# Attention with a routed expert layer on one core: k read in q's layout, full-row value products, and one timed list in place of a hand-ordered period

## The chip, the cores and the metric

The kernel is one program on one core of a Trainium2 chip. The metric is device time in microseconds (us). A core has a matmul engine (PE; its weight loads are PEld), a vector engine (DVE), an activation engine (ACT), a general engine (POOL) and a queue engine (SP). Each works through its own instructions strictly in program order and waits on semaphores for the others. DMAs are issued from SP, ACT and POOL and run on the core's 16 DMA engines.

## The reference

First a normalised attention over 8 batches of 12 heads, 448 positions, 64 channels, then a dense layer plus one chosen expert of eight for every token:

```python
q_n, k_n = rmsnorm(q, g_q), rmsnorm(k, g_k)          # over the 64 channels
scores = q_n @ k_n.T / sqrt(64)                       # per batch and head
attn = exp(scores) / sum(exp(scores))
x = (attn @ v) laid out as [8*448, 12*64]             # 3584 tokens x 768
y_dense = relu(x @ w1_dense) @ w2_dense               # 768 -> 512 -> 768
expert = argmax(x @ w_gate); gate = its softmax value
y = y_dense + gate * (relu(x @ w1[expert]) @ w2[expert])
```

The sum over keys does not depend on the order of the keys, as long as k and v are permuted alike.

## The kernel before, in words

**Groups and periods.** Four heads of a batch make a group `g`; there are 24 groups, three to a batch. `period(g)` holds the program of one group in seven steps `s`, and it works on several groups at once: the scores and exponentials of group g+1, the value products and divisions of group g, the PE transposes of k and q of group g+2, the norm statistics (14 `bn_stats` on DVE, L190) and the normalisation (4 products on POOL, L211) of group g+3, and loads of groups g+3 to g+6. In each step `scores` issues two to four matmuls (L247) and one exponential on ACT (L249, 896 values a partition), which sets the beat of the period. The PSUM tile of scores has two buffers, so ACT frees the place for the scores two steps on.

**Value products.** `attend(g, r, part)` multiplies the exponentials by the values for one half r of the group's heads. All its matmuls take 64 of the 128 rows; the two row halves alternate and write to different PSUM banks, and between part 0 and part 1 they change banks. `fenced()` puts a no-op on ACT there, which waits for part 0 and for which part 1 waits. The result lies in one PSUM tile, AV, which `division` (a reciprocal and two products on DVE, L313 and L309) must empty before the next `attend` starts.

**Loads.** q goes to partitions so that one partition holds seven neighbouring positions of a head (rows of 1792 bytes). k and v go in four DMAs for two groups, with three or four neighbouring positions a partition (rows of 768 and 1024 bytes), so that after the transposes each 128-key chunk of scores lies ready. All these loads are issued by SP. q has three buffers, k has two (each of two groups), v has one (of two groups); they lie in the space of the last five weight jobs (`LATE`), which are therefore loaded only when the attention's loads are over: all five in period 21, from POOL's queue.

**Routing.** When a batch is complete, `logits`, `choose`, `ranks`, `places` and `gates` find each token's expert and its place; `dense` and `relu` make the 512 hidden values of 128 tokens, and `scatter` (POOL, indirect DMA) writes the token's row to a table in device memory. PSUM tile W has two banks, shared by transposes, dense products, logits and ranks.

**Slot tiles.** The second part reads that table by experts, 128 slots a tile: `turn` loads a tile transposed (SP), `gemm1`, `htrans`, `gemm2` compute it on PE with ACT between, DVE copies the result (L677) and POOL scatters it to the output (L678). 14 tiles are known to be full after batch 5; `early_list` (20 small DVE instructions) finds them in one piece after period 20. After the last period `tail_and_slots` finishes the last two batches' work, makes the `final_list` and the `gaps`, and only then starts the tiles.

**Order.** Nothing reorders instructions: each engine's order is the order in which the Python code emits them.

Of the kernel before, what the change touches and what calls it, by code (L numbers as in the profile page):

```python
# [14 lines left out]
AX = mybir.AxisListType  # L15


@with_exitstack
def kernel(
# [92 lines left out]
    LATE, WPACE = 5, 1.75  # L112
    lflat = we.rearrange("p e a f -> p (e a f)")[:, -LATE * KD * F:]

    def lds(n, w):
        return lflat[:, n * 4 * S:(n + w) * 4 * S].bitcast(F32).rearrange("p (h s) -> p h s", h=2 * w)

    kls = [lds(0, 2), lds(2, 2)]
    qls = [lds(i, 1) for i in (4, 5, 6)]
# [21 lines left out]

    def load_q(g):
        if g < NG:
            xin["q", g] = qls[g % 3]
            nc.sync.dma_start(xin["q", g], q.rearrange("b h s d -> (b h) s d")[4 * g:4 * g + 4]
                              .rearrange("(i r) (p j) d -> (r p) i (j d)", r=2, j=J))

    def load_kv(x, src, g, n, engines):

        h = src.rearrange("b h s d -> (b h) s d")[4 * g:4 * (g + n)].rearrange(  # L150
            "(i r) s d -> r i s d", r=2)
        for r in range(2):
            for half in range(2):
                w = 4 if r == half else 3
                t0 = 0 if half == 0 else S - 64 * w
                c0 = 0 if r == 0 else S - w * D
                engines[(2 * r + half) % len(engines)].dma_start(
                    x[half * 64:half * 64 + 64, :, c0:c0 + w * D],
                    h[r][:, t0:t0 + 64 * w].rearrange("i (p t) d -> p i (t d)", t=w))

    def load_k(g):
        if g < NG:
            x = kls[g // 2 % 2]
            load_kv(x, k, g, 2, [nc.sync])
            for i in range(2):
                xin["k", g + i] = x[:, 2 * i:2 * i + 2]

    def load_v(g):
        if g < NG:
            load_kv(vls, v, g, 2, [nc.sync])  # L170
            for i in range(2):
                xin["v", g + i] = vls[:, 2 * i:2 * i + 2]
# [9 lines left out]
    def moments(g, name, s0, s1):  # L182
        weave(stats(g, name, s0, s1))
# [31 lines left out]
    def transposes(g):  # L215
        for n, name in enumerate("kq"):
            for s in range(J):
                c = S + (s if s < 3 else 6 if s == 3 else s - 1) * D if name == "k" else s * D
# [5 lines left out]

    def turned_q(g):
        qTs[g] = sb.tile([P, 2, S], BF16, tag="qT", name="qT")
        nc.vector.tensor_scalar(qTs[g], Wb[:, :, :S], gqk, None, op0=ALU.mult)

    def turned_k(g):

        kT = kTs[g % 2]
        nc.vector.tensor_copy(kT[:, :12 * D].rearrange("p (s c d) -> p c s d", c=2, d=D),
                              Wb[:, :, S:S + 6 * D].rearrange("p c (s d) -> p c s d", d=D))
        nc.vector.tensor_copy(kT[:, 12 * D:].rearrange("p (c d) -> p c d", d=D)[:, 0:3:2],
                              Wb[:, :, S + 6 * D:2 * S])

# [14 lines left out]
    def attend(g, r, part):  # L251


        va = vas[g % 3]
        if part == 1:
            fenced()
        full = (0, 1, 2) if r == 0 else (4, 5, 6)
        for s in full + (3,):
            for m in range(4):
                for half in range(2):  # L260
                    if s == 3 and half != r:
                        continue
                    hh = half ^ part
                    row = slice(half * 64, half * 64 + 64)
                    i = nc.tensor.matmul(  # L265
                        av[:, hh, m], exs[g, s][row, hh, QC[m]:QC[m] + P], va[row, s, hh, :De],
                        start=(part == 0 and s == full[0] and m == 0),
                        stop=(part == 1 and s == 3 if r == part else part == 1 and s == full[2]),
                        skip_group_check=True)
                    if part == 1 and fence[0]:  # L270
                        after(i, fence[0])
                        fence[0] = None
        if part == 0:
            fence[1] = i

    fence = [None, None]

    def fenced():
        if fence[1]:
            fence[0] = nc.scalar.nop()  # L280
            after(fence[0], fence[1])
            fence[1] = None

    def after(i, j):
        tc.add_manual_dep(i.ins, j.ins.name, mybir.DependencyInfo(
            mybir.DependencyClass.Sync, mybir.DependencyReason.DATA),
            reason="row tiles change banks")

    def weave(*works):

        works = [list(w) for w in works]
        while any(works):
            for w in works:
                if w:
                    w.pop(0)()

    def divide(g, r):
        weave(division(g, r))

    def division(g, r):  # L300
        b, gb = divmod(g, NB)
        if gb == 0 and r == 0:
            xas[b] = rb[b % 3][:, :, :XH].bitcast(BF16)
            xTs[b] = sb.tile([P, KD, S], BF16, tag="xT", name="xT")
        inv = sb.tile([P, 2, 4, 1], F32, tag="inv", name="inv")
        x = xas[b][:, :, gb * 256:gb * 256 + 256].rearrange("p m (a h i) -> p h m a i", a=2, h=4)

        def head(hh):
            nc.vector.tensor_tensor(  # L309
                x[:, 2 * hh + r], av[:, hh, :, :D].rearrange("p m (a i) -> p m a i", a=2),  # L310
                inv[:, hh].unsqueeze(3).to_broadcast([P, 4, 2, 32]), ALU.mult)

# [3 lines left out]
    def xtrans(g):  # L316
        b, gb = divmod(g, NB)
        for a in range(2):
# [4 lines left out]
    def xturned(g):  # L323
        b, gb = divmod(g, NB)
        nc.vector.tensor_copy(xTs[b][:, 2 * gb:2 * gb + 2],
                              Wb[:, 1, :2 * S].rearrange("p (a s) -> p a s", a=2))


    def logits(b):
# [154 lines left out]
    def dense(c, bank, k0, k1):  # L484
        b, m = divmod(c, 4)
        if b >= B:
            return
# [358 lines left out]
```

## Time and profile before

| | us |
|---|---|
| median of 3 runs (426.85 to 431.15) | 427.57 |
| the profiled execution | 427.64 |
| its span, first to last instruction | 425.9 |
| PE / DVE / ACT / POOL busy | 330.3 / 216.5 / 216.4 / 204.6 |
| first exponential of groups 0 and 2 | 17.3, 35.7 |
| last exponential | 249.7 |
| result copies of tile 1 and of the last tile (31) | 291.4, 413.7 |

A row of a group or of the timeline reads: source line, engine, operation, out<-in, shapes, count, then busy time and the mean of one, then the engine's idle time before it and what ended it. In the timeline the start and the length stand first, and neighbours of one kind are merged. A "q" after an engine's name means its sequencer, which issues DMAs. The ends of matmuls are modelled, so a row of n matmuls is longer by one matmul's latency than n times their pace.

### The profile page before, as it was taken

The numbers are of one execution on the slowest core, as the hardware profiler recorded it, in microseconds if no ns is written. First come the engines' busy times: TensorE is split into PE (matmuls) and PEld (weight loads), VectorE is DVE, ScalarE is ACT, GpSimd is POOL, SyncE is SP. The second block draws the span as 40 slices with busy tenths as digits, with TensorE's granted clock in tenths as the row PEclk, the third lists the DMA queues.
The fourth block names the chain that finished last, engine by engine and source line by source line (L and its number), as shares of the span: only waits on it lengthen the run. The fifth ranks groups of instructions, "written<-read, shape, count | busy, mean of one in ns | idle before, by whom it ended". The sixth has DMA issues, their size and how long they took to land. (4 is left out here: it accounts for less than half of the span.)

```text
span 425.9 us, 13310 instructions
## 1 busy us (share of the span) xinstructions
PE 330.3 (78%) x5170; PEld 200.7 (47%) x5219; DVE 216.5 (51%) x772; ACT 216.4 (51%) x345; POOL 204.6 (48%) x280
## 2 busy tenths in 40 slices
PE   0367777978878879779782876499999999999980
PEld 0135554554555545455451643135555555555540
DVE  4757686757877768587878343302212122221220
ACT  1287785966867868669772651113232232323310
POOL 2285585585677883857758312316322221212220
PEclk9998898979999989999998899969999999999996
DMA  6999988999698998799882996819978774765320
GB/s 188 244 214 270 232 197 210 245 260 215 147 307 214 254 244 196 206 226 212 235 177 72 199 208 184 199 55 222 198 182 181 177 168 117 149 167 155 96 114 32
DMA packets 91263, 80.58 MB, mean 189 GB/s; under 512 B 51516, under 2 KB 82748, under 8 KB 91200
## 3 DMA queue, kind: packets, MB, share of 16 engines
q1 hardware_dynamic: 78864, 43.44, 46.3%
q0 software_dynamic: 11440, 35.81, 31.7%
q8 instruction: 44, 0.72, 0.7%
q10 hardware_dynamic: 896, 0.46, 0.4%
q14 instruction: 19, 0.16, 0.1%
HBM read 61.40 MB, written 26.19 MB: 206 GB/s over the span
## 5 line engine op out<-in xcount | busy, mean ns | idle before, releaser
L249 ACT ACTIVATE xflat<-sc 128x896 bf16<-128x896 f32 x168 | 145.4, 917 | 30.2 <-PE sc L247 29.6
L211 POOL TENSOR_TENSOR xn<-we,r 128x448 bf16<-128x448 f32 x91 | 82.8, 940 | 23.2 <-issue 8.8
L247 PE MATMUL sc<-qT,kT 64*128 64x448 bf16 x384 | 76.2, 387 | 18.0 <-ACT xflat L249 15.8
L265 PE MATMUL AV<-va,xflat 64*128 64x65 bf16 x2688 | 67.9, 195 | 24.9 <-DVE rall L309 19.2
L677 DVE COPY xflat<-yp 128x768 f32<-128x768 f32 x32 | 30.6, 957 | 106.7 <-PE yp L671 106.7
L265 PEld LDWEIGHTS <-xflat 64*128 64x128 bf16 x2688 | 62.9, 98 | 42.4 <-issue 26.7
L678 POOL DMA_INDIRECT out_dram<-xflat,tail x32 | 31.3, 979 | 96.5 <-DVE xflat L677 91.5
L190 DVE BATCH_NORM_STATS2 st<-we 128x6 f32<-128x128 f32 x336 | 74.6, 276 | 4.8 <-DMA we<-in_k_dram 3.3
L661 ACT COPY heT<-AV 128x512 bf16<-128x512 bf16 x32 | 18.7, 585 | 68.1 <-PE AV L659 66.0
L489 PE MATMUL W<-wd,xT 128*128 128x512 bf16 x158 | 45.4, 395 | 8.0 <-issue 3.1
L649 PE MATMUL W<-we,xflat 128*128 x177 | 45.9, 396 | 4.1 <-DVE g L463 3.1
L391 POOL DMA_INDIRECT records<-rall,slot x32 | 32.8, 1024 | 31.7 <-ACT rall L497 21.6
L667 PE MATMUL yp<-wd,xflat 128*128 128x384 bf16 x256 | 47.6, 330 | 0.0
L671 PE MATMUL yp<-we,heT 128*128 x256 | 46.8, 326 | 0.0
L247 PEld LDWEIGHTS <-kT 64*128 64x128 bf16 x384 | 25.7, 96 | 42.9 <-issue 39.8
L653 ACT ACTIVATE hs<-W,tail 128x512 bf16<-128x512 f32 x32 | 22.0, 687 | 29.7 <-PE W L649 29.7
L309 DVE TENSOR_TENSOR rall<-AV,inv 128x256 bf16<-128x256 f32 x96 | 35.5, 411 | 0.4
L667 PEld LDWEIGHTS <-xflat 128*128 128x128 bf16 x256 | 25.3, 99 | 20.6 <-issue 1.4
L671 PEld LDWEIGHTS <-heT 128*128 128x128 bf16 x256 | 25.0, 98 | 16.6
L221 PE MATMUL W<-ident,xn 64*128 64x64 bf16 x672 | 18.5, 201 | 18.3 <-DVE gqk L730 13.1
L199 POOL TENSOR_TENSOR ss<-st,m 128x28 f32<-128x28 f32 x24 | 6.1, 253 | 50.5 <-ACT m L197 38.9
L221 PEld LDWEIGHTS <-xn 64*128 64x128 bf16 x672 | 17.2, 101 | 26.0 <-issue 18.5
(107 smaller groups left out, 296.1 us busy)
## 6 DMA issues: line engine op xcount, KB each, us to landing
we<-in_moe_w_dram POOLq DMA_DIRECT2D x16, 768.0 KB, 10.1
we<-in_q_dram SPq DMA_DIRECT2D x24, 448.0 KB, 5.9
vls<-in_v_dram SPq DMA_DIRECT2D x24, 256.0 KB, 8.3
we<-in_k_dram SPq DMA_DIRECT2D x22, 256.0 KB, 6.3
vls<-in_v_dram SPq DMA_DIRECT2D x24, 192.0 KB, 9.6
we<-in_k_dram SPq DMA_DIRECT2D x22, 192.0 KB, 8.1
wd<-in_moe_w_dense_dram POOLq DMA_DIRECT2D x2, 768.0 KB, 10.5
records<-rall,slot POOLq DMA_INDIRECT x32, 5.1
```

The lines of the kernel that those rows point to most:

```text
L190: return [lambda s=s: nc.vector.bn_stats(sts[g][:, "qk".index(name), s].rearrange("p h c -> p (h c)"), xin[name, g].rearrange("p h (s d) - ...
L211: (eng or nc.gpsimd).tensor_tensor(xn[name, g][:, :, hh], xin[name, g][:, hh].rearrange("p (s d) -> p s d", d=D), r[:, "qk".index(name), : ...
L221: nc.tensor.transpose(Wb[:, r, c:c + D], xn[name, g][half, s].rearrange("p h d -> p (h d)"), ident[half, half])
L247: nc.tensor.matmul(ps[:, hh, :S], kT[row, c:c + P], qT[row, r], start=(n == 0), stop=(n == len(mm) - 1), skip_group_check=True)
L249: nc.scalar.activation(x, ps[:, :, :S], AF.Exp, scale=scale)
L265: i = nc.tensor.matmul(av[:, hh, m], exs[g, s][row, hh, QC[m]:QC[m] + P], va[row, s, hh, :De], start=(part == 0 and s == full[0] and m == ...
L309: nc.vector.tensor_tensor(x[:, 2 * hh + r], av[:, hh, :, :D].rearrange("p m (a i) -> p m a i", a=2), inv[:, hh].unsqueeze(3).to_broadcast( ...
L391: i = nc.gpsimd.indirect_dma_start(out=rec, out_offset=bass.IndirectOffsetOnAxis(ap=slot[b % 2][:, m:m + 1], axis=0), in_=rb[b % 3][:, m], ...
L489: nc.tensor.matmul(W[:, bank], xTs[b][:, kk, QC[m]:QC[m] + P], wd1[:, kk], start=(kk == 0), stop=(kk == KD - 1))
L649: nc.tensor.matmul(he, xRs[t][:, kk], we[:, bass.ds(eregs[t], 1), 0, kk * F:(kk + 1) * F] .rearrange("p o f -> p (o f)"), start=(kk == 0), ...
L667: nc.tensor.matmul(yp[:, dd, :HD], xRs[t][:, KD + i], wd2[:, i, dd * HD:(dd + 1) * HD], start=(i == 0), stop=False)
L671: nc.tensor.matmul(yp[:, dd, :HD], heTs[t][:, i], we[:, bass.ds(eregs[t], 1), 1, i * Dm + dd * HD:i * Dm + (dd + 1) * HD] .rearrange("p o ...
```

## The change

Six things change together.

- **k** is loaded by `spread`, as q is: one DMA for two groups, rows of 1792 bytes. The transposes write k's columns in another order, so that `turned_k` copies contiguous runs. **v** keeps its four DMAs and its row lengths, but takes positions 0-3 and 4-6 (or 0-2 and 3-6) of a partition's seven, to match.
- **attend** uses full 128-row matmuls for three of the four key chunks and 64-row ones for the middle chunk. A call takes two of the four query chunks (m0 to m1); the parts, the bank change and ACT's no-ops are gone. 1536 matmuls stand where 2688 stood.
- **period** is gone. `attention` gives every operation of every group and batch a time in units of one step (seven to a period) out of a table `AT`, sorts the list, and emits it. What would come at or after the start of the last period's group (time 161) is left for the tail. The 14 statistics of a group come as one run, values are cast one group a period, and the loads of k, q and v are spread over two periods.
- **early_list** is spread: its 20 instructions get times 0.756 steps apart, among the other work of periods 20 to 22.
- **The late weights** are loaded one by one between times 133.9 and 149.2 (period 19 to 21), which the new places of the load buffers allow.
- **The tail** is a list too. The first three slot tiles (`TT = 3`) use the buffers of the scores instead of W and AV, and stand among the last period's value products and the last two batches' dense work. The final list and the gaps come in pieces of 8, 8 and the rest.

The prologue also becomes a list: k, q, k, q, q, k, v are loaded from SP alone, the gains from POOL, and ACT loads its table first.

```diff
+AT = dict(
+    p00=2.27, p01=0.85, d0=3.3, p10=5.96, p11=4.47, d1=6.6, xt=12.54, xe=13.5, tr=3.25, tq=3.67,
+    tk=3.65, va=3.13, st=(-0.01, 0.012), me=2.97, no=5.06, nm=(5.3, 0.272), kq='qk', lv=3.25,
...
+    def spread(x, src, g, n):
+        nc.sync.dma_start(x, src.rearrange("b h s d -> (b h) s d")[4 * g:4 * (g + n)]
+                          .rearrange("(i r) (p j) d -> (r p) i (j d)", r=2, j=J))
...
     def load_k(g):
         if g < NG:
             x = kls[g // 2 % 2]
-            load_kv(x, k, g, 2, [nc.sync])
+            spread(x, k, g, 2)
...
-    def attend(g, r, part):
-
+    def attend(g, r, m0, m1):
 
         va = vas[g % 3]
-        if part == 1:
-            fenced()
+        claim("av", ("av", g, r))
+        first = (g, r) not in begun
+        begun.add((g, r))
         full = (0, 1, 2) if r == 0 else (4, 5, 6)
...
+        row = slice(r * 64, r * 64 + 64)
+        for rows_, ss in ((slice(0, P), full), (row, (3,))):
+            for m in range(m0, m1):
+                for s in ss:
+                    for hh in range(2):
+                        nc.tensor.matmul(
+                            av[:, hh, m], exs[g, s][rows_, hh, QC[m]:QC[m] + P],
+                            va[rows_, s, hh, :De], start=(first and s == full[0] and m == m0),
+                            stop=(s == 3), skip_group_check=True)
...
+    def attention():
+        for g in range(NG):
+            z = J * g
+            if g:
+                for s in range(J):
+                    put1(z - J + s, ("s", g, s), scores, g, s)
+            for r in range(2):
+                for i, (m0, m1) in enumerate(((0, 2), (2, 4))):
+                    put1(z + AT["p%d%d" % (r, i)], ("p", g, r), attend, g, r, m0, m1)
+                put(shift(AT["d%d" % r], z), ("d", g, r), 3, lambda g=g, r=r: division(g, r))
...
+            if g > 2:
+                put(shift(AT["st"], z - 21), ("st", g), 14,
+                    lambda g=g: stats(g, "k", 0, 7) + stats(g, "q", 0, 7))
+                put1(z - 21 + AT["me"], ("me", g), means, g)
...
+            if g > 3 and g % 2 == 0:
+                put1(z - 14 + AT["lv"], ("lv", g), load_v, g)
+            if g > 4:
+                put1(z - 35 + AT["lq"], ("lq", g), load_q, g)
+                if g % 2 == 0:
+                    put1(z - 35 + AT["lk"], ("lk", g), load_k, g)
...
+        put(AT["el"], ("el",), 20, early_list)
+        todo.sort()
+        for t, _, key, f in todo:
+            if t < J * (NG - 1):
+                f()
+            else:
+                left.setdefault(key, []).append(f)
...
     def gemm1(t):
         row, n = place(t)
-        he = W[:, t % 2]
+        if t < TT:
+            mids[t] = psc.tile([P, 2, 512], F32, tag="sc", name="mid")
+            he = mids[t][:, 0]
+        else:
+            he = W[:, t % 2]
+            claim("01"[t % 2], ("he", t))
...
+        steps = {"tu": turn, "g1": gemm1, "ht": htrans, "g2": gemm2, "li": more}
+        for key in AT["tail"]:
+            if key[0] in steps:
+                steps[key[0]](*key[1:])
+            else:
+                do(key)
```

`put` and `put1` enter an operation with its time, `shift` moves a time by whole periods, `do` emits what was left under a key, and `claim` and `free` only assert while the program is built that a PSUM place has one user.

In the order of DVE in an ordinary period (no batch ends in it), before, from the first division of a period to its last:

```order
L313 RECIPROCAL inv<-AV 128x8
L190 BN_STATS st<-we 128x6
L309 TENSOR_TENSOR rall<-AV,inv 128x4x2x32 x2
L227 TENSOR_SCALAR qT<-W,gqk 128x896
L232 COPY kT_89<-W 128x2x6x64
L234 COPY kT_89<-W 128x2x64
L190 BN_STATS st<-we 128x6 x5
L325 COPY xT<-W 128x896
L313 RECIPROCAL inv<-AV 128x8
L190 BN_STATS st<-we 128x6
L309 TENSOR_TENSOR rall<-AV,inv 128x4x2x32 x2
L190 BN_STATS st<-we 128x6 x7
```

And in the changed kernel, the same stretch with the statistics at its head:

```order
L224 BN_STATS st<-we 128x6 x14
L342 RECIPROCAL inv<-AV 128x8
L336 TENSOR_TENSOR rall<-AV,inv 128x4x2x32 x2
L275 COPY kT_89<-W 128x768
L277 COPY kT_89<-W 128x2x64
L269 TENSOR_SCALAR qT<-W,gqk 128x896
L355 COPY xT<-W 128x896
L342 RECIPROCAL inv<-AV 128x8
L336 TENSOR_TENSOR rall<-AV,inv 128x4x2x32 x2
```

The 14 statistics, which lay between the divisions and copies, now follow the second division as one run, and k's copy precedes q's.

The early list on DVE, before, is one run between two divisions; its first rows are these (`ne`, `re`, `c`, `t`, `o` are its small tiles):

```order
L429 COPY ne<-W 1x8
L435 TENSOR_SCALAR re<-ne 1x8
L436 TENSOR_SCALAR re<-re 1x8
L410 TENSOR_TENSOR c<-re,erow 1x8
L411 SCALAR_TENSOR_TENSOR c<-onef,c 1x8
L412 MEMSET c 1x8
L413 COPY c<-erow 1x7
L414 TENSOR_TENSOR c<-c,re 1x8
L416 TENSOR_TENSOR t<-iot,c 1x112
```

In the changed kernel the same work (`u` are now its tiles) has the divisions and copies of the period between:

```order
L461 COPY u_4521<-W 1x8
L342 RECIPROCAL inv<-AV 128x8
L336 TENSOR_TENSOR rall<-AV,inv 128x4x2x32 x2
L275 COPY kT_88<-W 128x768
L277 COPY kT_88<-W 128x2x64
L269 TENSOR_SCALAR qT<-W,gqk 128x896
L466 TENSOR_SCALAR u_4522<-u_4521 1x8
L468 TENSOR_SCALAR u_4522<-u_4522 1x8
L444 TENSOR_TENSOR c<-u_4522,erow 1x8
L445 MEMSET c 1x8
L355 COPY xT<-W 128x896
L342 RECIPROCAL inv<-AV 128x8
```

What stood ahead of a division as a whole is now cut by three divisions and more.

In ACT's order at the end of the attention, before, all the dense work's `rall` rows come ahead of the first slot tile (`hs`, `heT`):

```order
L249 ACTIVATE xflat<-sc 128x896
L497 ACTIVATE rall<-W 128x512 x5
L363 ACTIVATE eg<-cent 128x32
L497 ACTIVATE rall<-W 128x512 x3
L653 ACTIVATE hs<-W,tail 128x512
L661 COPY heT<-AV 128x512
```

And in the changed kernel (`mid` is a buffer of the scores):

```order
L293 ACTIVATE xflat<-sc 128x896
L521 ACTIVATE rall<-W 128x512
L680 ACTIVATE hs<-mid,tail 128x512
L521 ACTIVATE rall<-W 128x512
L690 COPY heT<-mid 128x512
L521 ACTIVATE rall<-W 128x512
L680 ACTIVATE hs<-mid,tail 128x512
L690 COPY heT<-mid 128x512
L521 ACTIVATE rall<-W 128x512
L396 ACTIVATE eg<-cent 128x32
L521 ACTIVATE rall<-W 128x512
L680 ACTIVATE hs<-mid,tail 128x512
```

The two stages of tiles 0, 1 and 2 now stand between the last seven dense results.

More of the change, by code (lines that the diff above doesn't have):

```diff
@@ L144, in load_q @@
             xin["q", g] = qls[g % 3]
[L145 to L159, printed above, removed]
+            spread(xin["q", g], q, g, 1)
     def load_k(g):
@@ L249, in scores @@
         nc.scalar.activation(x, ps[:, :, :S], AF.Exp, scale=scale)
-    def attend(g, r, part):
+    begun = set()
+    def attend(g, r, m0, m1):
         va = vas[g % 3]
-        if part == 1:
-            fenced()
+        claim("av", ("av", g, r))
+        first = (g, r) not in begun
+        begun.add((g, r))
         full = (0, 1, 2) if r == 0 else (4, 5, 6)
[L258 to L295, printed above, removed]
@@ L401, with listed @@
     one = ctx.enter_context(tc.tile_pool(name="one", bufs=1))
-    def listed(n, per, first, last, row):
-        c = [one.tile([1, E], F32, name="c", tag=f"c{i}") for i in range(4)]
+    def listed(n, per, first, last, row, pre):
+        num, nxt, gap = [one.tile([1, E], F32, name="c", tag=f"c{i}") for i in range(3)]
         t = [one.tile([1, n, E], F32, name="t", tag=f"t{i}") for i in range(2)]
@@ L453, in final_list, with gaps @@
[L453 to L456 removed]
+        n, full, pre = [one.tile([1, E], F32, name=f"f{i}") for i in range(3)]
+        return [lambda: counted(B - 1, n)] + rounded(full, n, P, True) + listed(
+            NF, RT, used, full, 1, pre) + [lambda: nc.vector.tensor_copy(total, pre[:, E - 1:])]
+    def gaps(ix):
         cs = W[:, 0, :E]
[L459 removed]
@@ L620, with put, run, put1 @@
-    xRs, hes, heTs, eregs = {}, {}, {}, {}
+    todo, left = [], {}
+    def put(t, key, n, make):
+        got = []
+        def run(i):
+            if not got:
+                got.extend(make())
+                assert len(got) == n, (key, n, len(got))
+            got[i]()
+        t0, dt = t if isinstance(t, tuple) else (t, 0.001)
+        for i in range(n):
+            todo.append((t0 + i * dt, len(todo), key, lambda i=i: run(i)))
+    def put1(t, key, f, *a):
+        put(t, key, 1, lambda: [lambda: f(*a)])
@@ L769, in prologue @@
[L769 to L798 removed]
+        copies = {}
@@ new lines, in prologue, with more @@
+        for key in AT["pro"]:
+            steps[key[0]](*key[1:])
+    def tail_and_slots():
+        ix = one.tile([P, E], I32, name="gix")
+        lists = []
+        def more(n):
+            if not lists:
+                lists.extend(final_list() + gaps(ix))
+            for f in lists[:n]:
+                f()
+            del lists[:n]
+        steps = {"tu": turn, "g1": gemm1, "ht": htrans, "g2": gemm2, "li": more}
+        for key in AT["tail"]:
+            if key[0] in steps:
+                steps[key[0]](*key[1:])
+            else:
+                do(key)
+        assert not left and not lists, (left.keys(), len(lists))
+        gemm1(TT)
+        htrans(TT)
+        tiles(TT, NE + NL, ix)
@@ L800 @@
     with tc.manual_schedule(engines=ENGINES):
         prologue()
-        for g in range(NG):
-            period(g)
-            if g == NB * (FB + 2) - 1:
-                early_list()
+        attention()
         tail_and_slots()
```

451 lines of the change are left out of this document (182 added, 269 removed), and 21 rows, old and new, of tables (pro, tail).

## The prediction

> **What bounds the kernel now.** The chain of waits is no help: it holds two pieces, the last scatter. So the stages come first. The view of windows gives the busy time of each engine per stretch, then PE's granted clock, the DMA engines' share and GB/s.
>
> ```profile
> core 0: us, PE busy (x) PEld busy (x) DVE busy (x) ACT busy (x) POOL busy (x), PEclk, DMA share, GB/s
> 36.00:226.00 190.00, 152.56 (x3556) 97.96 (x3580) 139.98 (x547) 142.12 (x228) 128.90 (x178) 0.94 0.93 222
> 226.00:236.00 10.00, 2.63 (x52) 1.95 (x51) 7.52 (x22) 1.46 (x3) 9.53 (x14) 0.74 0.38 99
> 236.00:250.00 14.00, 11.84 (x296) 8.00 (x293) 6.57 (x22) 10.98 (x16) 3.51 (x6) 0.95 1.08 210
> 250.00:277.00 27.00, 15.75 (x208) 8.51 (x208) 9.88 (x49) 5.42 (x10) 7.99 (x9) 0.96 0.79 193
> 277.00:287.30 10.30, 9.32 (x36) 3.94 (x35) 0.27 (x2) 1.96 (x3) 1.96 (x2) 0.60 0.14 56
> 287.30:413.70 126.40, 125.55 (x785) 73.22 (x797) 29.70 (x32) 38.75 (x61) 36.24 (x37) 1.00 0.67 159
> ```
>
> Three kinds of stretch stand here. From 287.3 PE is full: the tiles are bound by matmuls, and nothing in the change touches their pace. From 226 to 287 no engine is full for long. From 36 to 226 the attention runs. The groups of lines in that window, and then its waits, say how long a period is and what it waits for.
>
> ```profile
> L249 ACT ACTIVATE xflat<-sc 128x896 bf16<-128x896 f32 x140 | 121.4, 917 | 18.9 <-PE sc L247 18.4
> L190 DVE BATCH_NORM_STATS2 st<-we 128x6 f32<-128x128 f32 x276 | 61.9, 276 | 0.0
> ACT m L197 <- DVE st L190: 21.5, 20, 1.8
> ACT xflat L249 <- PE sc L247: 18.4, 20, 1.8
> DVE inv L313 <- PE AV L265: 19.7, 27, 2.4
> DVE xT L325 <- PE W L489: 13.2, 17, 3.2
> POOL va L177 <- DMA vls<-in_v_dram: 2.3, 2, 2.0
> ```
>
> 140 exponentials are 20 periods in 190 us: 9.5 us a period, of which ACT works 142.12/20 = 7.1, DVE 7.0, POOL 6.4. So no engine sets the pace; ACT stands idle 2.4 us a period, and 21.5 + 18.4 of these 48 us have two causes: the squared means wait in ACT's order for the last statistics on DVE (once in each period), and the exponentials for scores that PE issues late, because PE in turn stands before value products whose place DVE has not emptied. This is a loop of waits, not a resource, with one exception: the DMA engines' share is 0.93, and 1.08 is what it reads when transfers never pause (236 to 250). At that rate the same transfers need 190 x 0.93/1.08/20 = 8.2 us a period. They are waited for little (2.3 us by POOL), since they are issued far ahead.
>
> The stall at 226 and the start of the tiles are read from the timeline (start, length, row):
>
> ```profile
> 226.45 0.86 DVE L436 TENSOR_SCALAR re<-re 1x8 f32<-1x8 f32 x1
> ...
> 234.02 0.93 PE L265 MATMUL AV<-va,xflat 64*128 64x65 bf16 x26 [7.37 <-DVE rall L309]
> ...
> 235.47 0.92 ACT L249 ACTIVATE xflat<-sc 128x896 bf16<-128x896 f32 x1 [8.54 <-PE sc L247]
> ...
> 249.72 0.92 ACT L249 ACTIVATE xflat<-sc 128x896 bf16<-128x896 f32 x1 [0.84 <-PE sc L247]
> ...
> 257.79 0.37 SPq L637 DMA_DIRECT2D tail<-records  x1
> ...
> 276.88 2.72 PE L649 MATMUL W<-we,xflat 128*128 x6 [3.08 <-DVE g L463]
> ...
> 287.54 1.24 PE L649 MATMUL W<-we,xflat 128*128 x5
> ...
> 291.42 0.96 DVE L677 COPY xflat<-yp 128x768 f32<-128x768 f32 x1 [3.16 <-PE yp L671]
> ...
> 295.54 0.96 DVE L677 COPY xflat<-yp 128x768 f32<-128x768 f32 x1 [3.16 <-PE yp L671]
> ```
>
> The early list holds a division back, the division holds PE for 7.37 us, and ACT loses 8.54. The first tile starts at 276.88, at about half the later pace (six matmuls in 2.72 against five in 1.24), and a tile takes 295.54 - 291.42 = 4.12 us from then on.
>
> **Part by part**, against the execution's own 427.64 us (span 425.9 and 1.74 around it; the median of the runs, 427.57, is the same).
>
> *Prologue.* These two rows set its length.
>
> ```profile
> 8.04 2.44 DVE L190 BATCH_NORM_STATS2 st<-we 128x6 f32<-128x128 f32 x12 [1.49 <-DMA we<-in_q_dram]
> 8.55 1.28 ACT L707 ACT_TABLE_LOAD   x1 [8.55 <-DMA gq<-in_g_q_dram]
> ```
>
> The first q no longer shares the engines with four loads of the second k, and the table no longer waits for the gains (8.55 + 1.28 = 9.83 was the earliest first mean). I take 2 us off. Bounds: 4 (q as early as the first k), and 2 lost, if the gains, now at the head of POOL's queue, land late and hold up the first copy of q.
>
> *A period.* PE's work first, since value products change their form. These rows give paces: 28 half-row products, eight 128-row transposes, 24 128-row products of 8 columns, and a dense product followed by scores.
>
> ```profile
> 118.13 0.65 PE L265 MATMUL AV<-va,xflat 64*128 64x65 bf16 x28
> 255.63 0.62 PE L320 MATMUL W<-ident,rall 128*128 128x128 bf16 x8
> 119.11 0.76 PE L333 MATMUL W<-wgb,xT 128*128 128x8 bf16 x24
> 248.72 0.59 PE L489 MATMUL W<-wd,xT 128*128 128x512 bf16 x2
> 249.25 0.36 PE L247 MATMUL sc<-qT,kT 64*128 64x448 bf16 x2
> 266.79 1.45 PE L489 MATMUL W<-wd,xT 128*128 128x512 bf16 x6 [0.35 <-DVE at L385]
> ```
>
> Less about 0.2 of latency at the end, a half-row product costs (0.65 - 0.2)/27 = 17 ns, 112 of them 1.9 us a group. Full rows appear in no row with 65 columns; between 8 columns ((0.76 - 0.17)/23 = 26 ns) and 128 ((0.62 - 0.22)/7 = 57 ns) they lie near 30, by columns. 48 full and 16 half are 48 x 30 + 16 x 17 = 1.7 us: 0.2 us less. But there are more changes between 64 and 128 rows. Dense products follow each other after (1.45 - 0.4)/5 = 0.21 us, so scores were due at 248.72 + 0.42 = 249.14 and came at 249.25: 0.1 us a change. The program has 115 changes before and 207 after, 92/24 = 3.8 more a group, or 0.4 us. In sum PE has nothing to gain, +0.2 us, hidden as long as a period is longer than PE's stream. The Trainium skill (TensorEngine Tiling (Array Packing), Key Properties) says that a change of tiling mode drains the engine; it gives no time, so the row's 0.1 stands.
>
> DVE and ACT do the same work; ACT's no-ops go. k's copy by contiguous runs I cost at nothing gained or lost. The 14 statistics (61.9/20 = 3.1 us a period) now precede the first division, so the means, after the third exponential in ACT's order, find them made, if the preceding division was on time. The loop that remains: means, one exponential, scores two steps on, the last value products, division, 14 statistics: 0.24 + 0.9 + 0.6 + 0.8 + 1.0 + 3.1 = 6.6 us (the first four by rows of this kind above, with latencies; estimates from the trace), below ACT's 7.1, so the wait of 21.5 should go for the most part. The wait for scores halves at best, because a PSUM place is still handed over twice a period. Transfers: k in longer rows can only be cheaper, I count nothing; 8.2 us stays the floor below which a period cannot stay. I take 8.5 us: 20 x (9.5 - 8.5) = 20 us. Bounds: 8.05 (ACT's 7.1 and half the remaining idle; the transfers 2% faster), 29 us; and 9.3, 4 us.
>
> *Early list.* Its 20 instructions meet other DVE work in periods 20 to 22, where no statistics are left after the first of them (3.1 us a period free against 7 us of list in two and a half periods). The 8.54 goes but for about 1.5: 7 us. Bounds 8.5 and 3, the latter if each piece waits behind a POOL product as L436 did (0.86).
>
> *Tail.* From the last exponential to the copy of tile 3 it takes 295.54 + 4.12 - 249.72 = 49.9 us now. PE's work in that stretch is the last group's value products 2, transposes 1.2, 44 dense products of 0.21 = 9.2, logits and ranks 1.1, and four tiles at 4.12 = 16.5: 30 us. In 250 to 277 PE idles 27 - 15.75 = 11.3 us; tile work between should fill a third or more. With 7.5 left the stretch takes 37.5: 12 us off. Bounds: 19 (nothing idle), and 3 (all idle time stays, with 4 us at the half pace and a wait for tile 0's rows). Tile 0's rows are on the path: the first `turn` started only at 257.79, behind scatters that stood in POOL's queue after five weight jobs. Now those jobs go one by one a period earlier, so the last scatter that tile 0 needs has about five steps, 6 us, to land before the tail begins.
>
> *Sum*: 2 + 20 + 7 + 12 = 41; 427.6 - 41 = **387 us**.
>
> **Rivals.** *Transfers set the period.* v has one buffer. Its load starts when the second group of a pair is cast, and the next cast comes 7 steps later in the new list, against 13 before.
>
> ```profile
> DMA to landing us min/median/max: 6.7/9.5/12.0
> ```
>
> That is the time to landing of each of v's DMAs in 36 to 226. 7 steps are 8.5 us at my period, with about 1.2 us of slack in POOL; at 12 the pair loses 2.3 us and the period is 9.3 or more with the queue behind it, SP's order putting k after v. Then 427.6 - 2 - 4 - 7 - 12 = 403. For it: a share of 0.93. Against: in the old list v queued behind k and q of the same step, now behind one q. Chance 0.18.
>
> *Weight loads show.* If a full-row product cannot load its weights under the one before, it costs 26 + 29 = 55 ns, 48 x 25 = 1.2 us more a period; PE, busy 152.56/20 = 7.6 us now (latencies included), goes to 9.0 with the changes of rows, and the period with it: 397 us. The eight transposes at 57 ns for 128 columns speak against it. The Trainium skill (TensorE: Matmul & The Clock Gate, Part 3) has weight loads overlap running matmuls only in other row groups, which would be this case; those transposes use the same rows and do not bear it out. Chance 0.08.
>
> *It fits better.* Period 8.1 and a tail with little idle: 427.6 - 3 - 28 - 8 - 14 = 375. The shortest periods before were about as short, but none twice running. Chance 0.2.
>
> *Slower: the run of statistics locks DVE to PE.* Before, single statistics filled the time in which DVE waited for value products. As one run they cannot, and if both divisions then wait the longest time in the row (2.4 us), a period is 7.0 + 4.8 = 11.8: 20 x 2.3 = 46 lost against 21 won elsewhere, 453 us. It decides from 10.6 us a period on. Against: value products are issued a step ahead of each division. Chance 0.05.
>
> *The tiles do not move.* Tile 0's rows land late, PE stands before `gemm1` in its order, and the last batch's work with it: the tail gains 0 and the sum is 399. Chance 0.05. The remaining 0.44 is the forecast, 380 to 394.
>
> **How the numbers follow.** Leaving a tenth out on each side, the range is 370 (period 8.05, the other terms between value and best bound: 427.6 - 3 - 29 - 8 - 17) to 406 (transfers at 9.3 and a tail that gains 8). About 1% can be told from no change. Faster by that much: all but the slower case and part of the last two, 0.92; within 1%: 0.03; slower: 0.05.
>
> **What would show it.** Right: about 8.5 us between groups of seven exponentials; means that wait under 0.4 us for statistics; no wait over 2 us on PE where the list was; the first gemm of a tile ahead of the last dense products at full pace; a tile still 4.12. Wrong: POOL's casts waiting for v by more than 1 us a pair, PE near full in the periods, or a wait over 3 us before the first tile's gemm, any of which moves the sum to its rival.

## The result and the profile after

The changed kernel takes **401.57 us** (median, 401.03 to 405.81), the kernel before beside it 427.21 (426.18 to 431.15): a ratio of 0.9405, interval 0.9318 to 0.9493. The forecast was 387 us. The profiled execution has a span of 400.0 us (before 425.9). A few executions below ran over 1.5% above their kernel's fastest; medians, ranges and ratios leave them out, and the profiles of experiments 6, 7 and 10 are of such executions.

The view of windows of the changed kernel, cut at the stages: 20 periods (from the first exponential of group 2 to that of group 22), the period of the early list, the last group up to its last exponential, and from there to tile 3's copy. The columns are those of the prediction's first fence.

```profile
core 0: us, PE busy (x) PEld busy (x) DVE busy (x) ACT busy (x) POOL busy (x), PEclk, DMA share, GB/s
33.80:216.20 182.40, 153.68 (x2617) 97.33 (x2638) 142.20 (x557) 143.34 (x230) 133.43 (x184) 0.94 0.94 239
216.20:223.40 7.20, 6.71 (x123) 4.43 (x123) 6.50 (x20) 6.37 (x10) 5.26 (x6) 1.00 1.04 270
223.40:233.70 10.30, 8.33 (x125) 5.26 (x124) 4.04 (x22) 6.00 (x10) 3.44 (x6) 0.83 0.80 180
233.70:273.30 39.60, 33.12 (x267) 19.09 (x273) 12.11 (x50) 11.47 (x19) 11.19 (x13) 1.00 0.62 156
```

The same boundaries in the trace of before lie at 35.7, 226.0, 241.8, 249.7 and 299.7. So the terms of the sum can be set beside what they measured, in one execution of each kernel:

| Stage | Before | After | Forecast | Measured |
|---|---|---|---|---|
| Up to group 2's first exponential | 35.7 | 33.8 | -2 | -1.9 |
| 20 periods | 190.3 | 182.4 | -20 | **-7.9** |
| Period of the early list | 15.8 | 7.2 | -7 | -8.6 |
| Last group to its last exponential | 7.9 | 10.3 | none | +2.4 |
| From there to tile 3's copy | 49.9 | 39.6 | -12 | -10.3 |
| The other tiles | 126.2 | 126.7 | 0 | +0.5 |
| Span | 425.9 | 400.0 | -41 | -25.9 |

Of the 15 us that are missing, 12 are missing in the periods: 9.12 us each in place of 8.5. Two other kernels with the same list in these periods (experiments 2 and 3) took 9.01 and 8.87, so this term is known to some 5 us. The waits in these 20 periods (engine, line, released by what: us in total, times, longest):

```profile
ACT xflat L293 <- PE sc L291: 34.9, 49, 2.2
POOL va L210 <- DMA vls<-in_v_dram: 26.9, 8, 5.3
...
PEld L256 <- POOL xn L245: 13.4, 12, 3.0
...
DVE inv L342 <- PE AV L309: 9.3, 8, 3.7
...
ACT m L231 <- DVE st L224: 0.3, 1, 0.3
```

The wait of the means for the statistics is gone (21.5 to 0.3), as forecast. In its place POOL waits 26.9 us for v, 8 times and up to 5.3 us, where it had waited 2.3. POOL's order has the four normalising products behind that cast, PE's order has the transposes behind these and scores behind the transposes; so ACT's wait for scores, which was to halve at best, went from 18.4 to 34.9. One such place in the timeline (start, length, row):

```profile
156.15 2.71 SPq L202 DMA_DIRECT2D vls<-in_v_dram  x4
...
167.10 1.10 POOL L210 CAST va<-vls 128x448 bf16<-128x448 f32 x2 [4.63 <-DMA vls<-in_v_dram]
...
168.16 3.64 POOL L245 TENSOR_TENSOR xn<-we,r 128x448 bf16<-128x448 f32 x4
...
169.26 1.73 ACT L293 ACTIVATE xflat<-sc 128x896 bf16<-128x896 f32 x2 [1.82 <-PE sc L291]
...
171.86 0.93 PE L256 MATMUL W<-ident,xn 64*128 64x64 bf16 x28 [0.70 <-POOL xn L245]
...
173.21 0.92 ACT L293 ACTIVATE xflat<-sc 128x896 bf16<-128x896 f32 x1 [1.09 <-PE sc L291]
```

From the first of v's four issues to the cast it takes 10.95 us. The view of v's tile says of what ("landing" is the time from a DMA's issue until its data are there):

```profile
L202 SPq DMA_DIRECT2D vls<-in_v_dram x37: 606/613/1396, 32.4 to 198.4; - x37
...
DMA to landing us min/median/max: 4.4/7.8/9.3
```

The last of four issues begins three issues of 0.61 us after the first, 1.8 us, and lands up to 9.3 us after that: up to 11.1 us, where seven steps of the forecast period give 8.5. The periods that begin with groups 5, 7, 9, 15, 17 and 19 take 9.9 to 13.4 us; those of 2 to 4, 10, 13 and 16 take 7.1 to 7.6.

The tail, on POOL and SP:

```profile
221.42 0.64 POOL L572 DMA_DIRECT2D we<-in_moe_w_dram  x1
225.09 1.08 POOL L210 CAST va<-vls 128x448 bf16<-128x448 f32 x2 [3.02 <-DMA vls<-in_v_dram]
226.33 1.01 POOL L424 DMA_INDIRECT records<-rall,slot  x1 [0.16 <-issue]
...
233.84 0.37 SPq L659 DMA_DIRECT2D tail<-records  x1
```

The last scatter that tile 0 needs stands behind one more late cast of v; POOL waits 3.02 us for it, in the last group. The tile's turn, which waits for that scatter, starts 7.5 us after its issue.

### The profile page after: what moved, and what is told of

It is laid out like the page before. It is cut to its first block, busy times and chain, and to the rows that moved or that the text cites. A ratio compares the mean times of both kernels' runs of the same rounds, so it can differ in the third digit from the quotient of the medians.

```text
span 400.0 us, 10925 instructions
## 1 busy us (share of the span) xinstructions
PE 328.4 (82%) x4024; PEld 199.8 (50%) x4067; DVE 214.4 (54%) x773; ACT 217.6 (54%) x345; POOL 205.6 (51%) x283
## 5 line engine op out<-in xcount | busy, mean ns | idle before, releaser
L309 PE MATMUL AV<-va,xflat 128*128 128x65 bf16 (+1 forms) x1536 | 78.1, 199 | 11.4 <-POOL va L210 6.5
L309 PEld LDWEIGHTS <-xflat 128*128 128x128 bf16 (+1 forms) x1536 | 63.2, 100 | 36.0 <-issue 22.1
L291 PE MATMUL sc<-qT,kT 64*128 64x448 bf16 x384 | 72.3, 383 | 10.1 <-ACT xflat L293 7.6
L224 DVE BATCH_NORM_STATS2 st<-we 128x6 f32<-128x128 f32 x336 | 68.3, 279 | 4.5 <-DMA we<-in_k_dram 3.1
L517 PE MATMUL W<-wd,xT 128*128 128x512 bf16 x163 | 47.5, 390 | 6.1 <-DVE qT L269 1.4
L210 POOL CAST va<-vls 128x448 bf16<-128x448 f32 x48 | 26.7, 586 | 29.9 <-DMA vls<-in_v_dram 29.9
L676 PE MATMUL W<-we,xflat 128*128 x160 | 39.6, 379 | 1.8 <-ACT rall L521 0.7
L256 PE MATMUL W<-ident,xn 64*128 64x64 bf16 x672 | 15.3, 197 | 21.2 <-DVE gqk L766 11.8
L517 PEld LDWEIGHTS <-xT 128*128 128x128 bf16 x192 | 17.2, 99 | 29.6 <-issue 16.0
L680 ACT ACTIVATE hs<-W,tail 128x512 bf16<-128x512 f32 x29 | 19.9, 687 | 21.9 <-PE W L676 20.6
## 6 DMA issues: line engine op xcount, KB each, us to landing
we<-in_moe_w_dram POOLq DMA_DIRECT2D x16, 768.0 KB, 10.3
```

The source lines that it names most:

```text
L224: return [lambda s=s: nc.vector.bn_stats(sts[g][:, "qk".index(name), s].rearrange("p h c -> p (h c)"), xin[name, g].rearrange("p h (s d) - ...
L291: nc.tensor.matmul(ps[:, hh, :S], kT[row, c:c + P], qT[row, r], start=(n == 0), stop=(n == len(mm) - 1), skip_group_check=True)
L309: nc.tensor.matmul(av[:, hh, m], exs[g, s][rows_, hh, QC[m]:QC[m] + P], va[rows_, s, hh, :De], start=(first and s == full[0] and m == m0), ...
L517: nc.tensor.matmul(W[:, bank], xTs[b][:, kk, QC[m]:QC[m] + P], wd1[:, kk], start=(kk == 0), stop=(kk == KD - 1))
L676: nc.tensor.matmul(he, xRs[t][:, kk], we[:, bass.ds(eregs[t], 1), 0, kk * F:(kk + 1) * F] .rearrange("p o f -> p (o f)"), start=(kk == 0), ...
```

## The experiments

The three groups of runs (1 to 4, 5 to 8, 9 to 11) were made on three chips, on which the kernel before took 429.75, 424.54 and 433.59 us. So ratios to before are compared between groups, and times only within one. Even the ratio is not the same on each chip: that of experiment 1 was 0.9104 and, repeated as experiment 9, 0.9193.

**1. v loaded ahead.** The rival "transfers set the period" named v's one buffer, which is a tile of its own and not in the space of the late weights. This run keeps every transfer and gives v time; the second group's cast moves 6.4 steps ahead for it, into the period of the first.

```diff
-    va=3.13, ..., lv=3.25,
+    va=3.13, ..., lv=-3.0,
...
-                put1(z - 7 + AT["va"], ("va", g), values, g)
+                put1(z - 7 + AT["va"] - (6.4 if g % 2 else 0), ("va", g), values, g)
```

> The values of both groups of a pair are cast in one period (the second group's cast 6.4 steps earlier) and v's load is issued 6.25 steps earlier, so that 13 steps and not 7 lie between the start of v's load and its first cast; the bytes moved, PE's, DVE's and ACT's work stay. Theory 'late v': POOL's wait for v falls from 26.9 us to under 5 us between 33 and 210 us, the period falls from 9.1 us to 8.0 to 8.6 us, and the time to 383 to 392 us. Rival 'transfers have no room left' (share 0.94): the wait goes to k, q or the weight loads instead, the period stays at 8.9 to 9.2 us and the time at 397 to 404 us. Rival 'a cast in the middle of POOL's normalising does the harm': POOL has two casts in one period, the period gets longer, 405 us or more.

Measured: 390.36 us (389.17 to 394.24), ratio 0.9104 (0.9034 to 0.9173). Windows of this run, the same stages:

```profile
35.80:205.30 169.50, 147.59 (x2622) 95.53 (x2642) 144.19 (x558) 142.80 (x230) 133.47 (x184) 0.99 1.02 259
...
212.50:220.20 7.70, 7.11 (x125) 4.71 (x124) 4.30 (x22) 5.77 (x9) 2.05 (x4) 1.00 1.00 219
220.20:262.90 42.70, 35.17 (x268) 19.52 (x274) 12.19 (x50) 11.48 (x19) 11.21 (x13) 0.92 0.58 146
```

And its waits in the 20 periods:

```profile
ACT xflat L293 <- PE sc L291: 21.8, 43, 2.9
...
POOL va L210 <- DMA vls<-in_v_dram: 3.9, 3, 2.2
```

POOL's wait for v falls from 26.9 to 3.9 us, ACT's for scores from 34.9 to 21.8, and a period to 169.5/20 = **8.47 us**, what the forecast had as a mean (the single periods run from 7.2 to 11.5). Beside experiments 2 and 3 on the same chip, whose 20 periods have v late and take 180.2 and 177.3 us, that is 8 to 11 us less. The DMA engines' share rises from 0.94 to 1.02: they carried the same transfers in 13 us less, so 0.94 was no limit. PE's granted clock differs too (0.94, here 0.99), but it does not order the periods: it is 0.97 in experiments 2, 8 and 6, where v has 7, 10.4 and 13 steps and the 20 periods take 180.2, 175.3 and 172.5 us. This is the lowest ratio of the study. The last group is back at 7.7 us. The tail is 3.1 us longer than in the changed kernel; experiment 6 says why.

**2. Tiles after the last batch's work.** `TT = 0`, and the tail's list without its tile steps.

```diff
-    tail=[('we', 18), ('d', 22, 1), ('tu', 0), ..., ('g1', 0), ..., ('ht', 0), ..., ('g2', 0, 0), ...
+    tail=[('we', 18), ('d', 22, 1), ('tu', 0), ...
...
-    TT = 3
+    TT = 0
```

> The three tiles' first and second gemms leave the list of the last batch and run after it, as before. If the tiles are what shortened the tail (from 49.9 to 39.6 us from the last exponential to tile 3's copy), the tail goes back to 48 to 51 us and the time to 410 to 413 us. If the spread early list and the earlier weight jobs did it (tile 0's rows ready earlier, the last batch's chain begun earlier), the tail stays below 44 us and the time below 406 us.

Measured: 405.38 us, ratio 0.9483 (0.9406 to 0.9561), against 0.9405. The time is within the second expectation (below 406), the tail in neither. In its timeline the last exponential and the copy of tile 3:

```profile
231.03 0.92 ACT L284 ACTIVATE xflat<-sc 128x896 bf16<-128x896 f32 x1 [1.28 <-PE sc L282]
...
276.60 0.96 DVE L701 COPY xflat<-yp 128x768 f32<-128x768 f32 x1 [3.16 <-PE yp L695]
```

The tail is 45.6 us here, 39.6 with the tiles between and 49.9 before: the tiles' place is worth 6.0 of the 10.3 us. The other 4.3 must come from what the tail finds done when it begins, which was not taken apart. The tail's start moves with the attention's end: last group and tail together take 57.8 us before, 49.9 in the changed kernel and 54.1 here, and counted so the tiles' place is worth 4.2 of 7.9.

**3. The early list in one run,** and **5. the same with v ahead.**

```diff
-    el=(143.16, 0.756),
+    el=(147.0, 0.001),
```

> The 20 instructions of the early list stand in one run again, at the place at which the last of them stood. If spreading them is what took the 8.6 us out of period 22, one exponential waits 7 us or more there again and the time is 408 to 410 us. If the stall had another cause (value products that come earlier now), the time stays within 2 us of 401.6.

Measured: 401.83 us, ratio 0.9374 (0.9316 to 0.9431): no loss. ACT in its timeline, where the list stands:

```profile
219.27 0.92 ACT L293 ACTIVATE xflat<-sc 128x896 bf16<-128x896 f32 x1 [1.60 <-PE sc L291]
221.56 1.73 ACT L293 ACTIVATE xflat<-sc 128x896 bf16<-128x896 f32 x2 [1.37 <-PE sc L291]
```

ACT loses 1.60 + 1.37 us there, not 8.54: that period takes 10.5 us in place of 7.2. The time did not rise because the 20 periods ahead of it took 8.87 us each, probably because v landed otherwise (POOL waited 23.9 us for it, not 26.9), so the run was repeated where v is on time.

> The kernel of the v experiment (v loaded 6.25 steps earlier, 390.4 us), and in it the early list's 20 instructions in one run again. In the run without the v edit the list in one run cost 3.3 us in period 22 (10.5 us against 7.2) and nothing in the sum, since the last exponential came earlier for other reasons. If that was luck of v's landings, the list in one run now costs what its period loses: 392.5 to 396 us. If what follows the last exponential makes up for it (tile 0's rows, not the attention, set the start of the tiles), the time stays at 389 to 392 us. By the prediction's term (7 us) it would be 397.

Measured: 392.55 us, ratio 0.9216 (0.9128 to 0.9304), against 0.9104 and 0.9193 (experiments 1 and 9) with the list spread, and on the edge between the two expectations. That period takes 10.8 us against 7.2, and the list delays the last scatter too; but what counts for the tiles, the turn, comes no later. POOL and SP in the timeline of this run, and then of experiment 1:

```profile
210.26 0.64 POOL L572 DMA_DIRECT2D we<-in_moe_w_dram  x1
...
218.34 1.03 POOL L424 DMA_INDIRECT records<-rall,slot  x1 [5.31 <-ACT rall L521]
...
222.32 0.37 SPq L659 DMA_DIRECT2D tail<-records  x1
```

```profile
210.52 0.63 POOL L572 DMA_DIRECT2D we<-in_moe_w_dram  x1
...
214.73 1.03 POOL L424 DMA_INDIRECT records<-rall,slot  x1 [1.43 <-ACT rall L521]
...
222.68 0.37 SPq L659 DMA_DIRECT2D tail<-records  x1
```

The scatter is issued 3.6 us later and the turn starts 0.4 us sooner: 12.1 and 12.2 us after the weight load ahead of the scatter, and 12.4 in the changed kernel (221.42 to 233.84). In the changed kernel's trace that load lands 11.4 us after its issue, 1 us before the turn. So the scatter is through just after the load ahead of it is, and spreading the list is worth some 3.5 us in its period, but in the sum only 1 to 5 us by the two ratios, with intervals that overlap.

**4. Only full rows, in the kernel before.** `attend` as in the change, the fences gone, everything else as before.

> The kernel before with one edit: value products over full 128 rows (and the order of places that goes with it), the two fences between its halves gone. By the prediction's sum (48 x 30 ns and 16 x 17 ns against 112 x 17 ns, and 3.8 more changes of rows a group at 0.1 us) PE gains nothing and the time stays within 1% of 427.6, at 424 to 431 us. If full rows are worth something by themselves (fewer matmuls for PE's sequencer, places emptied sooner), 420 us or less; if the weight loads or changes of rows show, 432 us or more.

Measured: 424.41 us, ratio 0.9873 (0.9818 to 0.9927): 1.3% faster, on the edge of what was expected. Its 20 periods take 184.2 us (37.4 to 221.6), 6 less, though PE's busy time in them rose from 152.86 to 157.71 us, the 0.2 us a period of the prediction's sum. Its waits there:

```profile
ACT m L197 <- DVE st L190: 21.5, 20, 1.7
...
ACT xflat L249 <- PE sc L247: 15.3, 21, 1.6
```

The means still wait 21.5 us for statistics: full rows have no part in that wait, and it stays as long as the order on DVE does. Whether the 6 us come from fewer matmuls, from the fences that are gone or from PE's granted clock (0.98 there, 0.94 before) was not separated.

**6. The late weights together,** with v ahead.

```diff
-    late=[137.84, 133.87, 140.49, 147.17, 149.18],
+    late=[148.3, 148.301, 148.302, 148.303, 148.304],
```

> The kernel of the v experiment, and in it the last five weight loads together at the end of the list's time (148.3) as in the kernel before, instead of one by one from 133.9 on. If they take the engines from the last scatters, or stand before them in POOL's queue, the first turn of tile 0 starts 3 us or more later (222.7 us there) and the time goes to 394 to 402 us. If they are far enough from the scatters, or give the attention's transfers room instead, 386 to 391 us.

Measured: 400.47 us (398.07 and 402.86), ratio 0.9406 (0.9293 to 0.9519), against 0.9104 and 0.9193 with the weights apart (experiments 1 and 9) and 0.9216 on the same chip (experiment 5, list in one): 8 to 13 us more, within the first of the two expectations. POOL, then SP, then PE in its timeline:

```profile
212.17 3.30 POOL L572 DMA_DIRECT2D we<-in_moe_w_dram  x5
215.76 1.06 POOL L424 DMA_INDIRECT records<-rall,slot  x1 [0.30 <-issue]
...
219.18 1.02 POOL L424 DMA_INDIRECT records<-rall,slot  x1 [0.18 <-issue]
```

```profile
237.45 0.37 SPq L659 DMA_DIRECT2D tail<-records  x1
```

```profile
241.54 2.72 PE L676 MATMUL mid<-we,xflat 128*128 x6 [12.75 <-DMA xflat<-records]
```

The turn starts 18.3 us after the last scatter's issue, and PE stands 12.75 us before the first gemm. In the kernel before, too, the scatters stood behind five loads together, and the prediction's timeline holds the turn:

```profile
232.57 3.26 POOL L540 DMA_DIRECT2D we<-in_moe_w_dram  x5
...
237.16 1.06 POOL L391 DMA_INDIRECT records<-rall,slot  x1 [0.22 <-issue]
...
245.81 1.06 POOL L391 DMA_INDIRECT records<-rall,slot  x1 [7.30 <-ACT rall L497]
```

The scatter of 237.16 lands 19.6 us after its issue. The last one that tile 0 needs there is that of 245.81, which ACT's dense work released: 12.0 us to the turn at 257.79. In the changed kernel it is 7.5. With v ahead it is 8.0 (above), and PE waits before the first gemm:

```profile
226.81 2.72 PE L676 MATMUL mid<-we,xflat 128*128 x6 [2.33 <-DMA xflat<-records]
```

The attention now ends 2 us sooner after that scatter, and this wait is most of the 3.1 us by which the tail of experiment 1 is longer. In the second profile of that kernel (experiment 9) the turn starts 1.2 us before the last exponential, and the tail is 40.3 us. So the tail's gain stands on the weights, not on the tiles alone: with tiles between but weights together it is gone. From the last exponential at 224.5 to the turn it takes 13 us here (8.1 before, 0.1 in the changed kernel), and the tail is 53.4 us.

**7. k in short rows,** with v ahead, and **9, 10. the base (the kernel of experiment 1) and this edit again.** Two DMAs for a pair of groups, with rows of 1024 and 768 bytes, put the same values in the same places.

```diff
-            spread(x, k, g, 2)
+            for c0, c1 in ((0, 4), (4, 7)):
+                nc.sync.dma_start(x[:, :, c0 * D:c1 * D], ...[:, :, c0:c1]...)
```

> The kernel of the v experiment (share of the DMA engines 1.02), and in it k's loads of a pair split into two, of rows of 1024 and 768 bytes in place of 1792, for the same bytes. If the transfers now bound the period at 8.47 us, shorter rows lengthen it: 394 us or more. If transfers have slack there, or the length of these rows is without effect, 389 to 392 us, and the prediction's nothing for k's longer rows stands.

> The v experiment once more, so that the two runs beside this one have it on the same chip. By its first run: 0.910 of the time of before, 387 to 393 us.

> The v experiment with k's rows of 1024 and 768 bytes once more, beside its own base. If transfers bound the period after v is loaded ahead, it is 3 us or more slower than the base; if k's longer rows are worth nothing, as the prediction counted, within 2 us.

Measured: 394.01 us (391.55 to 395.14; 0.9244, 0.9164 to 0.9324) in the second group, which has no base of its own. In the third, 403.55 us (399.53 to 404.47; 0.9292, 0.9218 to 0.9366) beside a base of 398.52 (397.25 to 399.80; 0.9193, 0.9132 to 0.9253), where this chip's before took 433.59. The base itself missed what was expected of it (0.910, 387 to 393 us): the edit of experiment 1 is worth about 1% less on this chip. Short rows cost about 1% twice, 5 us beside their own base, with intervals that overlap. So k's long rows are probably worth a few us once v is ahead; whether by their length or by one issue fewer is open.

**8. Between.** The second cast 3.8 steps earlier, v's load 3.55 (`lv=-0.3`).

> The second group of a pair casts v 3.8 steps earlier than in the changed kernel, behind the four normalising products and not between them and the mean (6.4 steps earlier in the v experiment), and v's load is issued 3.55 steps earlier: 10.4 steps from load to cast, between 7 (401.6 us) and 13 (390.4 us). If the distance from load to cast is what counts, POOL waits for v 8 to 18 us and the time is 393 to 398 us. If 10.4 steps are enough and the two casts in one place hold the normalising up, the time is below 390 us.

Measured: 397.19 us (396.00 to 398.75), ratio 0.9335 (0.9258 to 0.9411), as expected if the distance counts. Its row of waits for v in the 20 periods:

```profile
POOL va L210 <- DMA vls<-in_v_dram: 17.0, 7, 5.4
```

Wait, period and ratio go together: 7 steps, 26.9 us, 9.12 us, 0.9405; 10.4 steps, 17.0, 8.76, 0.9335; 13 steps, 3.9, 8.47, 0.9104. On the chip of this run, experiment 5 has 13 steps in the same periods: 0.6 us of wait and 8.45 us. But v is not all that sets the period: experiment 9, on the third chip, waits 1.1 us for v and its period is 8.76.

**11. The last two weight jobs behind the scatter,** with v ahead.

```diff
-    late=[137.84, 133.87, 140.49, 147.17, 149.18],
+    late=[137.84, 133.87, 140.49, 154.70, 154.90],
```

> The v experiment, and in it the last two weight loads behind the last scatter that tile 0 needs, not 9 and 4 us ahead of it. If a scatter's landing waits for the weight loads ahead of it in POOL's queue, it lands in 4 to 6 us and not 7.9, the first turn starts 2 to 4 us earlier, and the time falls to 385 to 388 us, unless the weights, two steps later, are now what the first gemm waits for (then 390 to 393 us). If the landing depends on what the scatter moves alone, no change: within 1 us of the base.

Measured: 400.84 us (398.80 to 404.23; 0.9261, 0.9188 to 0.9335) beside the base of 398.52: no gain. POOL, SP and PE:

```profile
218.43 0.98 POOL L424 DMA_INDIRECT records<-rall,slot  x1 [4.85 <-ACT rall L521]
219.41 1.44 POOL L572 DMA_DIRECT2D we<-in_moe_w_dram  x2
```

```profile
221.68 0.37 SPq L659 DMA_DIRECT2D tail<-records  x1
222.26 5.60 SPq L660 DMA_TRANSPOSE xflat<-records  x1
```

```profile
232.17 2.21 PE L676 MATMUL mid<-we,xflat 128*128 x5 [3.82 <-DMA tail<-records]
```

And SP and PE of the base:

```profile
226.84 0.37 SPq L659 DMA_DIRECT2D tail<-records  x1
227.42 1.44 SPq L660 DMA_TRANSPOSE xflat<-records  x1
...
233.31 1.46 PE L676 MATMUL mid<-we,xflat 128*128 x6 [1.32 <-ACT rall L521]
```

With nothing near ahead of it the scatter is through in 3.3 us (4.8 in the base). But the weights now run beside the tile's own loads: the second of them takes 5.60 us to issue (1.44 in the base), the first gemm starts 10.5 us after the turn (6.5 in the base), and it waits for these loads, where in the base it waits for ACT. The wait moved by one place.

## Why the prediction was right and wrong

**The period** is the term that was mis-sized: -20 forecast, -7.9 measured, 9.12 us and not 8.5. The step that failed is "They are waited for little (2.3 us by POOL), since they are issued far ahead", a reading of the old list that was kept as the main case for the new one. In the new list POOL waits 26.9 us. The rival "transfers set the period" had the mechanism, v's one buffer and 7 steps for 13, and with 403 us nearly the result, while 401.57 lies outside the main case's 380 to 394. It got 0.18, on the argument that v now queues behind one q only. That its time came so near is partly luck: its own loss of 2.3 us a pair makes the period 8.5 + 1.15 = 9.65 us, not 9.3, and the sum about 410; measured are 2.7 us a pair, of which not all reaches the period. The landing counted in the rival, 9.5 us in the middle and 12 at most, was rather shorter after (7.8 and 9.3); what was left out is that this time runs from each DMA's own issue, and the fourth is issued 1.8 us after the first. The sum "landing plus issues against seven steps", 11 us against 8.5, could have been made from the profile of before and speaks for the rival as the likeliest case. In experiment 1, with v ahead, the period is 8.47, and the kernel at 390.36 is 3 us from the forecast; experiment 8 lies between, as that reading has it. That the mean then meets 8.5 so closely is in part luck: it is 8.76 on another chip, and what makes the periods of groups 9 and 19 last 10.1 and 11.5 us with v ahead is open. (The best bound, 8.05, comes from the transfers alone; ACT's 7.1 and half of the idle time left without the means' wait, 1.3, would be 7.8.)

**The loop of waits** went as argued: means 21.5 to 0.3 us, and experiment 4, which leaves the order of the statistics as it was, keeps the 21.5. Moving the statistics alone was not tried. The wait for scores did not halve; with v ahead it is 21.8 (27.5 in experiment 9), no less than before (18.4), perhaps because the place in PSUM still changes hands twice a period, as the prediction said, and because PE waits for normalised k and q; that was not tested.

**PE's work** was right: +0.2 us a period in the sum, +0.24 in experiment 4, and 153.68 us in 20 periods after against 152.86. A full-row product was put near 30 ns; in the timeline of the changed kernel twelve in a row:

```profile
232.64 0.54 PE L309 MATMUL AV<-va,xflat 128*128 128x65 bf16 x12
```

(0.54 - 0.2)/11 = 31 ns. "Weight loads show" (55 ns) falls. The rule that the prediction weighed from the Trainium skill (TensorE: Matmul & The Clock Gate, Part 3) does not hold for these products: they use the same rows one after the other, and at 31 ns their loads are hidden. What "nothing to gain" missed is experiment 4: in a kernel with that form, and without the fences, the old periods took 6 us less at no less PE work.

**The early list**: -7 forecast, -8.6 measured, but only in part for the reason given. In one run in the new list it costs 3.3 to 3.6 us of its period, so more than half of the old stall of 8.54 did not come from the run as such but from the order around it, and little of what spreading saves reaches the end, since tile 0's rows set the start of the tiles.

**The tail**: -12 forecast, -10.3 measured. "Tile work between should fill" PE's idle time is worth 6.0 (experiment 2); the weights matter more, which the prediction named as a condition only ("about five steps, 6 us, to land"; 7.5 measured). Without that condition the kernel of experiment 1 loses 8 to 13 us (experiment 6). In the sum, 7.5 us of PE's idle time were to be left beside 30 us of work; measured are 6.5 and 33.1. The prediction's own numbers leave 19.9 us beside that work (49.9 - 30); it reads 11.3 of them as idle, fills a third of these, and lets the other 8.6 go without a reason. "The tiles do not move" fell, but its cause, late rows of tile 0, is what bounds the tail as soon as the attention is faster.

**The prologue** (-1.9 for -2) proves little: with the same new prologue group 2's first exponential stands between 33.8 and 37.0 us in the eleven profiles, and with the old one at 35.7 and 37.4. The tiles' pace (4.12 us as before) was right. "Slower: the run of statistics locks DVE to PE" fell: DVE's wait for value products went down, 19.7 to 9.3 us. The last group's +2.4 was not priced; POOL waits there for v once more (3.02 us).

## What to carry to other kernels

When a schedule is shortened, recompute for every single-buffered transfer the time from its buffer's release to its next use, and set it against the number of issues times the issue time plus the landing of the last: a wait that is small in the old order says nothing of the new one. A DMA that something soon waits for must not stand behind large ones that nobody waits for yet, in its queue or on the shared engines. And a saving ahead of a join is worth only what the other branch of the join allows: measure where the join is before sizing the term.

## What was not expected of the hardware

- Behind five weight loads of 768 KB in POOL's queue, a scatter of 128 rows is through 19.6 us after its issue in the kernel before, and the turn that waits for it starts 18.3 us after it in experiment 6; with no load near it is 3.3 us. Behind one or two loads, the turn starts 10.9 to 12.8 us after the last load's issue in nine profiles, whether the scatter was issued 4 or 8 us after that load (4.2 to 8.6). The Trainium skill (DMA: Bandwidth & Descriptors, Two DMAs through the same engine are not ordered) has descriptors of one queue of a DMA engine start in order; these times agree.
- Another queue is no way round: in experiment 11, beside weights issued by POOL, the tile's second load from SP took 5.60 us to issue, and 1.44 in the base. The Trainium skill (DMA: Bandwidth & Descriptors, Issuing engines are not separate DMA queues) has the DMAs of all issuers interleave on the same 16 engines, and this run agrees.
- A DMA share of 0.94 over the periods left room: the same transfers ran at 1.02 when v was issued earlier.
- One kernel (before) took 424.54 to 433.59 us on three chips, and the ratio of the edit of experiment 1 was 0.910 and 0.919 on two of them. That spread is as large as several of the terms above.
